# A scored with landmarks on the rows, its fold turned by DMA, and row-tiled products

## The chip, the cores and the metric

The kernel runs on one core of one Trainium2 chip. The metric is the time of one execution on the device in microseconds (us). Runs more than 1.5% above the fastest of the same kernel are called slow. PE is TensorE, ACT is ScalarE, DVE is VectorE, POOL is GpSimd, SP is the engine that issues most DMAs here. "Granted clock" is the share of PE's full clock that the profile shows as granted. SBUF is the memory that tiles lie in, PSUM the one that PE writes its products to. "The chain that ended last" is the work followed back from the last instruction, at each step to what it had waited for.

## The reference, cut to what matters

```python
# q, k, v: (8 batches, 8 heads, 576 rows, 64); m = 32 landmarks, each the mean of 18 rows
A  = softmax(scale * q    @ k_lm.T)      # 576 x 32 per head
Bm = softmax(scale * q_lm @ k_lm.T)      # 32 x 32
C  = softmax(scale * q_lm @ k.T)         # 32 x 576
Z  = six Newton steps towards the inverse of Bm
x  = A @ Z @ C @ v                       # heads side by side: 576 x 512 per batch
x1, x2, x3 = split(x @ w_proj)
y  = x1 * irfft(rfft(x2) * filter) * x3  # the transform runs along the 576 rows
out = y @ w_out
```

The transform of x2 is taken on A itself, 256 columns per batch (8 heads of 32), which is smaller than x2. The transform is split into even and odd frequencies, so it needs the sum and the difference of rows s and s+288 of A: the "fold". A is therefore needed twice: with rows s on the partitions, folded (AE, weights of the DFT), and turned, with (head, landmark) on the partitions (AT, for the products with G).

## The kernel before

It forms A with the rows on the partitions, 96 rows to a tile, and turns it on PE. Cuts are marked.

```python
def back(b):
    def scores(cc, src, t, dst):                       # 512 columns: 2 chunks x 8 heads x 32
        pc = ktile("pc")                               # PSUM, two buffers
        ...                                            # eight products of 64 columns
        nc.scalar.activation(dst[:, 2*cc:2*cc+2, :].rearrange("p c l -> p (c l)"),
                             pc[:R, :], AF.Exp, bias=0.0, scale=scale)
    for cc in range(3):
        scores(cc, qT, 0, eA)
        nc.vector.tensor_reduce(rA[...], eA[...], axis=AX.X, op=ALU.add)
        scores(cc, kT, 1, eC)
    ...                                                # 1/rA, A = eA * (1/rA), C @ v
    nc.vector.tensor_tensor(AE[:, 0], A[:, 0:3], A[:, 3:6], op=ALU.add)       # the fold
    nc.vector.tensor_tensor(AE[:, 1], A[:, 0:3], A[:, 3:6], op=ALU.subtract)
    ...
    for g in range(2):                                 # A turned on PE
        pt = ktile("ptA", F16)
        for c in range(NC):                            # NC = 6
            mm(pt[:, c*R:(c+1)*R], A[:, c, 128*g:128*g+128], identh[:R, :R], is_transpose=True, ...)
        nc.vector.tensor_copy(AT[:, g, :], pt[:, :S])

def gate(b, after):
    ...                                                # DFT, G = ZC @ w_proj, X, Y
    def conv(j, EO):                                   # three full products a parity
        for par in range(2):
            pi = wtile()
            for t in range(2):
                mm(pi[:, 0:HS], Y[:, par, t, P*j:P*j+P], IV[:, par, t, :], start=(t == 0), stop=False)
            mm(pi[:, 0:HS], Y2[:, P*(j%2):P*(j%2)+P], IV2[:, j//2, par, :], start=False, stop=True)
            nc.scalar.copy(EO[:, par, j%2], pi[:, 0:HS])
```

A batch passes a front (landmark means, first products), six Newton steps, `back` (above), and the gate; the instructions of up to four batches are woven together. Below, "front stretch" is the time in which fronts, scores, Newton steps and DFTs run, and "gate stretch" the rest of a batch.

The softmax here doesn't subtract the row's maximum and nothing guards it: scores larger than these inputs give would overflow.

Of the kernel before, what the change touches and what calls it, by code (L numbers as in the profile page):

```python
# [8 lines left out]
F32 = mybir.dt.float32  # L9
BF16 = mybir.dt.bfloat16  # L10
# [10 lines left out]
def kernel(  # L21
# [10 lines left out]
    nc = tc.nc  # L32
# [7 lines left out]
    NC = S // R  # L40
    HS = S // 2
    TW = HS + 16

    NPE = 2
    consts = ctx.enter_context(tc.tile_pool(name="consts", bufs=1))
# [39 lines left out]
    def load_q(b):  # L85
        qn = io.tile([R, H, NC, D], BF16, tag="qn", name="qn")
        for e in range(2):
            nc.gpsimd.dma_start(
                qn[:, :, 3 * e:3 * e + 3, :].rearrange("p h c d -> p h (c d)"),
                q[b].rearrange("h (e p c) d -> e p h (c d)", e=2, c=3)[e])  # L90
        loaded[b].append(qn)

    def load_v(b):
        vn = vbufs[b % NV]
        for i in range(2):
            nc.gpsimd.dma_start(  # L96
                vn[:, :, i].rearrange("p x c d -> p x (c d)"),
                v[b].rearrange("(x h) (p c) d -> h p x (c d)", h=2, c=NC)[i])
        vloaded[b] = vn

    def load(b):
# [5 lines left out]
    kc = big.tile([R, 2, TW], F32, tag="y", name="kc")  # L107
    nc.gpsimd.iota(kc[:, :, 0:P], pattern=[[1, 2], [2, P]], base=0, channel_multiplier=0,
                   allow_small_or_imprecise_dtypes=True)
    nrow = consts.tile([R, 3], F32, name="nrow")  # L110
    nc.gpsimd.iota(nrow, pattern=[[1, 3]], base=0, channel_multiplier=3,
                   allow_small_or_imprecise_dtypes=True)
    load_q(0)
# [8 lines left out]
    poolq = consts.tile([R, 16], BF16, name="poolq")  # L122
    nc.vector.memset(poolq, 1.0)
    select(poolq, [[-6, 16]], ALU.is_ge, 0.0, 0, 1)
    select(poolq, [[6, 16]], ALU.is_ge, 0.0, 5, -1)

# [7 lines left out]
    lmbufs = [consts.tile([P, 2, H, 2, m], BF16, name=f"lm{i}") for i in range(NL)]  # L134
# [5 lines left out]
    for tb in tbufs:  # L140
        for x in tb:
            nc.vector.memset(x[:, 24 * R:], 0.0)
    IV2 = consts.tile([P, 2, 2, HS], F16, name="IV2")

# [9 lines left out]
    for lb in lmbufs[1:]:  # L154
        fill(lb.rearrange("p t h c l -> p (t h c l)"), 4 * H * m, 0.0)
    fill(IV2.rearrange("p x y s -> p (x y s)"), 4 * HS, 0.0)
    off = big.tile([R, 2, TW], F32, tag="y", name="off")
# [6 lines left out]
    J = consts.tile([P, 2, 64], F16, name="J")  # L164
    JH = consts.tile([P, 2, 2, 64], F16, name="JH")
    mask2 = consts.tile([P, 2], F32, name="mask2")
    nc.vector.memset(J, 0.0)
    nc.vector.memset(mask2, 1.0)
    select(J, [[0, 2], [-1, 64]], ALU.not_equal, 1.0, 0, 1)
    select(J, [[0, 2], [-1, 64]], ALU.not_equal, 1.0, -64, 1)  # L170
    select(mask2, [[-64, 2]], ALU.is_ge, 0.0, 0, 1)
    select(mask2, [[64, 2]], ALU.is_ge, 0.0, 63, -1)
    for e in range(2):
        nc.vector.tensor_scalar(JH[:, e], J, mask2[:, e:e + 1], None, op0=ALU.mult)
# [5 lines left out]
    nc.vector.tensor_copy(blk4, mask4.unsqueeze(2).to_broadcast([P, 4, 32]))  # L180
    identh = consts.tile([P, P], F16, name="identh")
# [4 lines left out]
    def load_w(i):  # L186
# [3 lines left out]
    filt = big.tile([R, 2, 3, Dm], BF16, tag="G", name="filt")  # L190
    nc.gpsimd.dma_start(filt.rearrange("p e c j -> p e (c j)"),
                        moe_filter_fft.rearrange("(e p c) j -> p e (c j)", e=2, c=3))
# [3 lines left out]
    F = consts.tile([R, 3, 2, TW], F16, name="F")  # L196
    Ft = consts.tile([R, 3, 2, 2, 2, 16], F16, name="Ft")
# [4 lines left out]
    def tables_fwd():  # L202
# [5 lines left out]
        for c in range(3):  # L208
            t = big.tile([R, 2, TW], F32, tag="T", name="t", bufs=1)
            nc.vector.scalar_tensor_tensor(t, in0=kc, scalar=nrow[:, c:c + 1],  # L210
                                           in1=off, op0=ALU.mult, op1=ALU.add)
            u = big.tile([R, 2, TW], F32, tag="X", name="u")
# [25 lines left out]

    def front(b):
        kn, qn = loaded[b]  # L240
        lm = lmbufs[b % NL]
# [3 lines left out]
        for h in range(H):  # L245
            for cc in range(3):
                x = mm(pk[:, h * m:(h + 1) * m],  # L247
                       kn[:, h, 2 * cc:2 * cc + 2, :].rearrange("p c d -> p (c d)"),
                       poolk, start=(cc == 0), stop=(cc == 2), skip_group_check=True)
                if b in pins:  # L250
                    tc.keep_in_program_order(x)
        yield
        pq = ftile("pq")
        pq3 = pq[:, 0:384].rearrange("p (x h l) -> p x h l", x=3, h=H)
        for h in range(H):
            for cc in range(3):
                x = mm(pq3[:, cc, h, :],  # L257
                       qn[:, h, 2 * cc:2 * cc + 2, :].rearrange("p c d -> p (c d)"),
                       poolq, start=True, stop=True, skip_group_check=True)
                if b in pins:  # L260
                    tc.keep_in_program_order(x)
        Pk = sm.tile([P, H, m], F16, tag="Pk", name="Pk")
        nc.scalar.activation(Pk.rearrange("p h l -> p (h l)"), pk[:, 0:256], AF.Copy,
                             bias=0.0, scale=1.0 / blk)
        Pq = sm.tile([P, 3, H * 16], F16, tag="Pq", name="Pq")
        nc.scalar.activation(Pq.rearrange("p x l -> p (x l)"), pq[:, 0:384], AF.Copy,
                             bias=0.0, scale=1.0 / blk)
        yield
        pj = ftile("pj")
        pj4 = pj.rearrange("p (t h l) -> p t h l", t=2, h=H)  # L270
        Jf = J.rearrange("p a d -> p (a d)")
        mm(pj[:, 0:256], Jf, Pk.rearrange("p h l -> p (h l)"), start=True, stop=True,
           skip_group_check=True)
        for e in range(2):
            dst = pj4[:, 1, :, 16 * e:16 * e + 16]
            mm(dst, Jf, Pq[:, 2 * e, :], start=True, stop=False, skip_group_check=True)
            mm(dst, JH[:, e].rearrange("p a d -> p (a d)"), Pq[:, 1, :],
               start=False, stop=True, skip_group_check=True)
        nc.vector.tensor_copy(lm[0:64, :, :, 0, :], pj4[0:64])
        nc.scalar.copy(lm[64:128, :, :, 1, :], pj4[64:128])  # L280
# [6 lines left out]
        for g in range(2):  # L287
            for hh in range(4):
                h = 4 * g + hh
                mm(B2[32 * hh:32 * hh + 32, g, :], lm[0:64, 1, h, 0, :], lm[0:64, 0, h, 0, :],  # L290
                   start=True, stop=True, skip_group_check=True)
# [84 lines left out]
    def back(b):  # L376
        vn = vloaded.pop(b)
        lm = lmbufs[b % NL]
        kT, qT = tbufs[b % 2]

        def scores(cc, src, t, dst):
            pc = ktile("pc")
            pc4 = pc.rearrange("p (c h l) -> p c h l", c=2, h=H)
            for h in range(H):
                mm(pc4[:, :, h, :], src[:, (3 * h + cc) * R:(3 * h + cc) * R + P],  # L385
                   lm[:, t, h, :, :].rearrange("p c l -> p (c l)"),
                   start=True, stop=True, skip_group_check=True)
            nc.scalar.activation(dst[:, 2 * cc:2 * cc + 2, :].rearrange("p c l -> p (c l)"),  # L388
                                 pc[:R, :], AF.Exp, bias=0.0, scale=scale)

        eC = big.tile([R, NC, 256], BF16, tag="eC", name="eC", bufs=1)
        eA = big.tile([R, NC, 256], BF16, tag="eA", name="eA", bufs=1)
        rA = sm.tile([R, NC * H], F32, tag="rA", name="rA")
        for cc in range(3):
            scores(cc, qT, 0, eA)
            nc.vector.tensor_reduce(  # L396
                rA[:, 2 * H * cc:2 * H * (cc + 1)],
                eA[:, 2 * cc:2 * cc + 2].rearrange("p c (h l) -> p (c h) l", l=m),
                axis=AX.X, op=ALU.add)
            yield  # L400
            scores(cc, kT, 1, eC)
            yield


        nc.vector.reciprocal(rA, rA)
        rA2 = sm.tile([R, NC * H, 2], BF16, tag="rA2", name="rA2")
        nc.vector.tensor_copy(rA2, rA.unsqueeze(2).to_broadcast([R, NC * H, 2]))
        A = big.tile([R, NC, 256], F16, tag="A", name="A", bufs=1)
        nc.vector.tensor_tensor(
            A.rearrange("p c (h a t) -> p (c h) a t", a=16, t=2),  # L410
            eA.rearrange("p c (h a t) -> p (c h) a t", a=16, t=2),
            rA2.unsqueeze(2).to_broadcast([R, NC * H, 16, 2]), op=ALU.mult)
# [4 lines left out]
        for g in range(2):  # L417
            pv = ktile("pv")
            for c in range(NC):
                for x in range(2):  # L420
                    mm(pv[64 * x:64 * x + 64, 0:192],  # L421
                       eC[:, c, 128 * g + 64 * x:128 * g + 64 * x + 64],
                       vn[:, 2 * g + x, :, c, :], start=(c == 0), stop=(c == NC - 1),
# [10 lines left out]
        AE = big.tile([R, 2, 3, 256], F16, tag="AE", name="AE")  # L434
        nc.vector.tensor_tensor(AE[:, 0], A[:, 0:3], A[:, 3:6], op=ALU.add)
        nc.vector.tensor_tensor(AE[:, 1], A[:, 0:3], A[:, 3:6], op=ALU.subtract)
        att[b] = dict(AE=AE)
        yield
        pz = ktile("pz")
        RZ = solved.pop(b)  # L440
        pz4 = pz[:, 0:128].rearrange("p (x l) -> p x l", x=4)
        for g in range(2):
            for pp in range(2):
# [380 lines left out]
```

## Time and profile before

| kernel before | |
|---|---|
| time | 240.7 us median of 3 runs (240.68 to 240.97) |
| span of the profiled run, mean granted clock | 241.6 us, 0.961 |
| first factor product (G with AT) of batches 0 to 7, us from the start | 52.4, 81.9, 110.5, 135.5, 160.0, 184.5, 206.4, 223.2 |
| steps between them | 29.5, 28.5, 25.1, 24.5, 24.5, 21.9, 16.8 |

The steps are the clearest measure of a batch. The last ones have less of a next batch to prepare, so 16.8 us is a gate nearly alone.

Three windows of the kernel before: a front stretch, three steady batches, a gate nearly alone. After the window come its length and the busy time of each engine.

```profile
core 0: us, PE busy (x) PEld busy (x) DVE busy (x) ACT busy (x) POOL busy (x), PEclk, DMA share, GB/s
117.60:126.80 9.20, 8.88 (x163) 6.25 (x162) 7.22 (x22) 7.41 (x20) 2.30 (x3) 1.00 1.08 221
110.50:184.70 74.20, 73.62 (x880) 44.62 (x880) 60.42 (x158) 63.03 (x142) 4.98 (x7) 1.00 0.95 144
206.40:223.20 16.80, 16.72 (x129) 9.02 (x129) 10.72 (x18) 14.95 (x33) 0.00 (x0) 1.00 0.27 71
```

PE is busy 73.62 of 74.20 us.

Groups of instructions of the kernel before (busy us, mean ns of one, then idle time of the engine before them):

```profile
L396 DVE TENSOR_REDUCE rA<-eA 96x16 f32<-96x512 bf16 x24 | 16.2, 677 | 3.0 <-ACT eA L388 2.8
L388 ACT ACTIVATE eA<-pc 96x512 bf16<-96x512 f32 x24 | 14.6, 607 | 0.4 <-PE pc L385 0.3
...
L409 DVE TENSOR_TENSOR A<-eA,rA 96x1536 f16<-96x1536 bf16 x8 | 7.6, 947 | 0.0
L462 DVE COPY AT<-ptA 128x576 f16<-128x576 f16 x16 | 7.2, 447 | 3.9 <-PE ptA L460 3.9
L460 PE MATMUL ptA<-identh,A 96*128 96x96 f16 x96 | 7.0, 215 | 0.0
```

These are what the change takes out or replaces. The exp of A takes 607 ns for 512 columns.

What a change of PE's tile mode costs is seen in the chain of the kernel before. Its columns are start, length, engine, tile and line, and how many instructions.

```profile
126.77 0.55 PE w L537 x4
127.32 0.97 PE w L680 x4
...
129.51 0.86 PE w L680 x4
...
132.36 0.55 PE w L583 x16
132.91 0.97 PE w L680 x4
```

Four full 512-column products take 0.86 us among their own kind and 0.97 behind 64-column (L537) or 32-column (L583) products: 0.11 us for each change of mode.

### The profile page before, as it was taken

The page shows a single profiled execution, that of the slowest core. Times are in us where ns is not written, and L with a number is a line of the kernel's source. Part 1 is how long each engine was busy: PE and PEld are TensorE (multiplying, and loading weights), DVE is VectorE, ACT ScalarE, POOL GpSimd, SP SyncE. Part 2 cuts the span into 40 slices and gives each one's busy share as a digit, 9 for nine tenths or more (in the row PEclk, how much of TensorE's full clock was granted, in tenths as well). Part 3 has the DMA queues.
Part 4 walks back from the last instruction along what each step waited for, and adds up shares of the span by engine and source line. Part 5 has one row for each costly group of instructions (what it writes and reads, how often), then busy time and mean ns, then how long its engine had stood idle before and what let it go on. Part 6 is the DMA issues. An engine that isn't in the chain of part 4 may idle for free.

```text
span 241.6 us, 6421 instructions
## 1 busy us (share of the span) xinstructions
PE 223.4 (92%) x2547; PEld 134.6 (56%) x2547; DVE 182.4 (75%) x478; ACT 185.8 (77%) x407; POOL 37.7 (16%) x62
## 2 busy tenths in 40 slices
PE   7959769999999999999999999999999999999980
PEld 3537434666665667645754576457645664554630
DVE  8936943579978989896879777977797789567540
ACT  8663525888879878888878888788878987898850
POOL 7962310012203321040032001100000000000000
PEclk9967965999999999999999999999999999999998
DMA  5999999949999999999999996995015004305115
GB/s 73 195 210 196 208 202 198 172 80 176 165 149 167 218 196 154 177 191 146 171 217 140 165 230 152 115 157 173 3 47 152 0 3 107 89 4 150 48 42 153
DMA packets 61998, 33.78 MB, mean 140 GB/s; under 512 B 42320, under 2 KB 57680, under 8 KB 61968
## 3 DMA queue, kind: packets, MB, share of 16 engines
q0 software_dynamic: 27536, 16.85, 53.7%
q1 hardware_dynamic: 34432, 16.52, 36.1%
q8 instruction: 20, 0.33, 0.6%
q14 instruction: 10, 0.08, 0.1%
HBM read 33.69 MB, written 9.44 MB: 178 GB/s over the span
## 4 chain that ended last, share of the span: by engine, by line
PE 78%; DVE 9%; ACT 9%; issue 1%; DVEq 0%; ACTq 0%
PE w L612 12%; PE w L680 11%; PE w L639 6%; PE w L568 6%; PE w L537 6%; PE w L547 5%; PE pc L385 4%; PE pv L421 4%; PE pn L362 3%; PE w L641 3%; PE pq L257 2%; PE ptA L460 2%; PE w L504 2%; PE w L583 2%; PE pk L247 2%; ACT EO L643 2%
## 5 line engine op out<-in xcount | busy, mean ns | idle before, releaser
L680 PE MATMUL w<-wout,y 128*128 128x512 bf16 x128 | 33.4, 380 | 0.4 <-DVE y L658 0.4
L612 PE MATMUL w<-AT,G 128*128 128x512 f16 x128 | 32.8, 380 | 0.2
L541 ACT CAST G<-w 128x512 bf16<-128x512 f32 x48 | 25.5, 597 | 4.0 <-PE w L537 3.9
L617 DVE TENSOR_TENSOR gt<-w,x 128x512 bf16<-128x512 f32 x32 | 21.6, 685 | 9.0 <-ACT x L615 5.0
L643 ACT CAST EO<-w 128x288 bf16<-128x288 f32 x64 | 24.1, 403 | 2.8 <-PE w L641 2.8
L682 ACT COPY os<-w 128x512 f32<-128x512 f32 x32 | 18.5, 589 | 8.9 <-PE w L680 8.3
L639 PE MATMUL w<-IV,Y 128*128 128x288 f16 x128 | 25.0, 286 | 0.3 <-ACT EO L643 0.3
L573 DVE TENSOR_TENSOR T<-X,HH 128x2048 bf16<-128x2048 bf16 x16 | 19.5, 1220 | 7.1 <-ACT X L570 6.4
L615 ACT CAST x<-w 128x512 bf16<-128x512 f32 x32 | 19.0, 599 | 2.9 <-PE w L612 2.4
L537 PE MATMUL w<-wproj,ZC 128*64 128x512 bf16 x96 | 19.4, 400 | 0.0
L547 PE MATMUL w<-F,AE 96*128 96x304 f16 x96 | 19.2, 313 | 0.1
L680 PEld LDWEIGHTS <-y 128*128 128x128 bf16 x128 | 11.0, 97 | 14.5 <-issue 4.2
L570 ACT CAST X<-w 128x512 bf16<-128x512 f32 x32 | 17.9, 592 | 1.4 <-PE w L568 0.9
L396 DVE TENSOR_REDUCE rA<-eA 96x16 f32<-96x512 bf16 x24 | 16.2, 677 | 3.0 <-ACT eA L388 2.8
L641 PE MATMUL w<-IV,Y 128*128 128x288 f16 x64 | 18.3, 286 | 0.0
L568 PE MATMUL w<-G,Ah 128*128 128x512 bf16 x64 | 18.0, 382 | 0.0
L612 PEld LDWEIGHTS <-G 128*128 128x128 bf16 x128 | 11.0, 97 | 12.5 <-ACT G L541 4.0
L366 ACT CAST RZ<-pn 128x256 f16<-128x256 f32 x40 | 15.4, 386 | 2.8 <-PE pn L362 1.8
L96 POOL DMA_DIRECT2D vb<-in_v_dram x16 | 10.8, 678 | 41.0 <-PE w L547 25.1
L549 ACT CAST Ah<-w 128x304 f16<-128x304 f32 x32 | 12.8, 421 | 4.3 <-PE w L547 4.2
L362 PE MATMUL pn<-RZ 128*128 128x160 f16 (+1 forms) x96 | 13.7, 223 | 2.3 <-DVE RZ L367 1.7
L729 PE MATMUL w<-zero 128*128 128x512 bf16 (+1 forms) x55 | 14.2, 398 | 1.4 <-DVE zero L138 1.4
(152 smaller groups left out, 472.4 us busy)
## 6 DMA issues: line engine op xcount, KB each, us to landing
kn<-in_k_dram POOLq DMA_DIRECT2D x8, 576.0 KB, 9.7
qn<-in_q_dram POOLq DMA_DIRECT2D x16, 288.0 KB, 11.5
vb<-in_v_dram POOLq DMA_DIRECT2D x16, 288.0 KB, 9.7
out_dram<-os SPq DMA_DIRECT2D x24, 192.0 KB, 2.5
out_dram<-os SPq DMA_DIRECT2D x16, 128.0 KB, 2.4
wproj<-in_moe_w_proj_dram POOLq DMA_DIRECT2D x3, 512.0 KB, 14.8
out_dram<-os SPq DMA_DIRECT2D x24, 64.0 KB, 2.1
out_dram<-o SPq DMA_DIRECT2D x16, 64.0 KB, 2.1
```

Of the source, the lines that this page charges most:

```text
L362: mm(pn2[:, g, lo:160], RZ[:, g, 0:128], RZ[:, g, lo:160], start=True, stop=True, skip_group_check=True)
L537: mm(pg[64 * pp:64 * pp + 64, :], part["ZC"][:, 2 * g + pp, :, :].rearrange("p h l -> p (h l)"), wparts[jb][:, 2 * g + pp, :], start=True, ...
L541: nc.scalar.copy(G[:, g, Dm * jb:Dm * (jb + 1)], pg)
L547: mm(pf[:, 0:TW], part["AE"][:, par, c, 128 * g:128 * g + 128], F[:, c, par, :], start=(c == 0), stop=(c == 2))
L568: mm(px, Ah[:, g, par, 128 * t:128 * t + 128], G[:, g, Dm:2 * Dm], start=(g == 0), stop=(g == 1))
L573: nc.vector.tensor_tensor(T, X.unsqueeze(2).to_broadcast([P, 2, 2, Dm]), HH[:, par], op=ALU.mult)
L612: mm(px, G[:, g, lo:lo + P], part["AT"][:, g, 0:512], start=(g == 0), stop=(g == 1))
L617: nc.vector.tensor_tensor(gt[:, j, 0:512], px, x1, op=ALU.mult)
L639: mm(pi[:, 0:HS], Y[:, par, t, P * j:P * j + P], IV[:, par, t, :], start=(t == 0), stop=False)
L641: mm(pi[:, 0:HS], Y2[:, P * (j % 2):P * (j % 2) + P], IV2[:, j // 2, par, :], start=False, stop=True)
L643: nc.scalar.copy(EO[:, par, j % 2], pi[:, 0:HS])
L680: mm(po, y[:, j, i0:i0 + P], wout[:, j, :], start=(j == 0), stop=(j == 3))
```

## The change

The intent: make the scores of A directly with (head, landmark) on the rows, so that no PE transpose and no wide DVE reduction is needed. Row sums and the spreading of their reciprocals become small PE products. The fold becomes sums and differences of the two halves of a row of AT, and only the folded A is turned, by DMA, from the second batch on. Products that use 32 or 64 of the array's rows are tiled by rows, so that several can run together. The core of the diff, with cuts marked:

```diff
-        for e in range(2):
-            nc.gpsimd.dma_start(qn[:, :, 3*e:3*e+3, :]..., q[b].rearrange("h (e p c) d -> ...", e=2, c=3)[e])
+        nc.gpsimd.dma_start(qn..., q[b].rearrange("h (p c) d -> p h (c d)", c=NC))
 ...
+        def scores_a(g):
+            pa = [ktile("pa") for _ in range(2)]
+            for pos in range(4):
+                for c2 in range(2):
+                    h = head(g, pos)
+                    mm(pa[c2][32*pos:32*pos+32, 0:HS], la[64*c2:64*c2+64, h, :],
+                       qT[64*c2:64*c2+64, h*HS:(h+1)*HS], ...)
+            for c2 in range(2):
+                nc.scalar.activation(eA[:, g].rearrange("p (r c x) -> p c x r", x=2, c=3)[:, :, c2, :],
+                                     pa[c2][:, 0:HS].rearrange("p (c r) -> p c r", r=R),
+                                     AF.Exp, bias=0.0, scale=scale)
 ...
+        # row sums: pr[...] = SU x eA, twelve 32-column products; rA2 = 1/pr
+        for g in range(2):
+            pb = [ktile("pb") for _ in range(2)]
+            ...            # pb = SB x rA2, six products of 32 rows
+            for c2 in range(2):
+                view = lambda t: t[:, g].rearrange("p (c x r) -> p c x r", x=2, r=R)[:, :, c2, :]
+                nc.vector.tensor_tensor(view(AT), view(eA), pb[c2]..., op=ALU.mult)
+        ...                # At = AT[:, :, 0:288] +- AT[:, :, 288:576]
+        if b >= NPA:       # NPA = 1
+            nc.sync.dma_start_transpose(AE, At)
+        else:
+            ...            # nine PE transposes, two copies
 ...
         def conv(j, EO):
+            pi = [wtile() for _ in range(2)]
             for par in range(2):
                 for t in range(2):
                     mm(pi[par][:, 0:HS], Y[:, par, t, ...], IV[:, par, t, :], start=(t == 0), stop=False)
-                mm(pi[:, 0:HS], Y2[:, ...], IV2[:, j//2, par, :], start=False, stop=True)
+            for par in range(2):
+                p0 = 64*(j//2) + 32*par
+                mm(pi[par][:, 0:HS], Y2[p0:p0+32, ...], IV2[p0:p0+32, :], start=False, stop=True)
 ...
-            store(i0, P, os)                   # rows 3p+c of each half
+            nc.sync.dma_start(out[b, i0:i0+P, :], os)
```

The DFT's last 32 rows become row-tiled products like those of conv, G is made of eight tiles of 64 rows by 32 columns, and the landmark means of 512-column products. The order of rows changes too: q now comes as rows 6p+c, and the columns of A are put back into natural order.

## The prediction

> **What bounds it now.** The page gives TensorE (PE) 92% busy, ScalarE (ACT) 77%, VectorE (DVE) 75%, DMA at nine tenths for two thirds of the span; the chain of waits that ended last is 78% PE, 9% DVE, 9% ACT. From the timeline: 62 us for the first batch, then some 24.5 us a batch (first L612 at 110.5, 135.7, 160.2, 184.7), 16.8 us for the last ones, which have no next batch to prepare. The window of three steady batches (110.5 to 184.7) shows PE busy 73.6 of 74.2 us, ACT 63.0, DVE 60.4. In its gate stretch, about 16 us, PE issues back to back; in the front stretch (117.6 to 126.8: pooling, scores, Newton, DFT) the products' own spacing sums to about 7 of 9 us and the chain goes PE to ACT and back.
>
> **What the change does, per batch.**
> DVE: out go row-sum reduction (3x677 ns), reciprocal and copy (437+201), A product (947), fold (543+546), AT copies (2x447), masked ZC (418), lm (680): 6.7 us. In come a reciprocal (est. 0.75), four 288-column products from PSUM (est. 0.46 each, between the 425 ns of 256 and the 685 of 512), folds (est. 1.15), ZC, lm and small ones: est. 5.0. Saves 1.7.
> ACT: exp of A from 3x607 to 4x403 (the 128x288 copy); Pk, Pq, lm (385+492+581) become Pk and la (est. 590+371). Saves 0.7.
> PE: matmuls of different column groups already start 3 ns apart in the trace (64-column pairs, 32-column fours), and each change of column mode costs about 106 ns (the 512-column matmul lands 322 ns after a tiled one, 216 after its own kind). [...] So g_part falls from about 0.65 to 0.44 us, three times (-0.6); twelve A transposes of 43 ns go (-0.5); pooling with 512-column products, pj, row sums, spreading of the reciprocals and pz add about 1.5, mostly switches. Conv (24 products of 122 ns to 20 slots) and DFT (12 of 130 to 10) save 0.75 if row-tiled pairs run together and the switch between full and row-tiled is free, as 96-row and 128-row ones mix freely now[...]. Net PE: between -0.4 and +1.3 us.
> DMA: q comes in half as many packets; each AE transpose (seven, 295 KB) has a whole gate to land in.
>
> **On the critical path.** The gate stretch gains from g_part and the removed transposes until ACT (14.9 of 16.8 us at the end) stops it. The front stretch gains through ACT and DVE, and loses PE's switches. I estimate 0.5 to 0.8 us less for each of six batches, 1 at the start, 1 to 2 at the end: about 6 us.
>
> **Predicted:** 235 us, 8 in 10 between 228 and 244. Faster by over 2%: 0.54; within 2%: 0.33; slower: 0.13.
>
> **What would show it.** DVE busy near 170 us, ACT near 178; PE as busy as now; the step from batch to batch near 23.8; row-tiled conv pairs ending some 3 ns apart; no chain piece waiting for the AE transpose.
>
> **What would make it wrong.** [...] pairs of PSUM buffers taken at once that make PE wait for both exps; AE transposes queued behind stores; or a front stretch bound by ACT's chain more than I think, so that 228 comes out.

The 106 ns are from the trace. The bad case of the row-tiled products: if a change between full and row-tiled products costs what a change of column mode does, conv and DFT lose 0.5 us a batch instead of saving 0.75, and the time is about 240 us or more. The sum: per batch 1.7 us saved on DVE, 0.7 on ACT, between -0.4 and +1.3 on PE (plus is time added); on the critical path 0.5 to 0.8 us for each of six batches, 1 at the start and 1 to 2 at the end, about 6 us, from 240.7 to 235.

That 96-row and 128-row products mix freely is in the trace of the kernel before: from 110 us on, a 512-column product lands 217 to 219 ns after a 96-row one and 216 after its own kind. Where an estimate names no line, its working is not on record. The same trace has, to set beside them: a reciprocal of 1 column 148 ns and of 48 columns 437 (the 0.75 us is for 96), the folds 543 and 546 ns (the 1.15 us), ACT copies of 512 columns 592 ns and of 256 columns 371 (the 590 and 371 ns). The 0.44 us for g_part and the 1.5 us that PE adds are estimates.

## More of the kernel before

The page of the kernel before: busy time of each engine, the granted clock in 40 equal slices (tenths of full speed), and the chain that ended last.

```profile
PE 223.4 (92%) x2547; PEld 134.6 (56%) x2547; DVE 182.4 (75%) x478; ACT 185.8 (77%) x407; POOL 37.7 (16%) x62
...
PEclk9967965999999999999999999999999999999998
...
PE 78%; DVE 9%; ACT 9%; issue 1%; DVEq 0%; ACTq 0%
```

PE sets the pace, and from the eighth slice on its clock is full (1.00 from 42 to 241 us).

## The result and the profile after

The changed kernel took 306.36 us (median of 4 runs, 305.79 to 320.39), the kernel before 240.83 us beside it. Over fast runs the ratio is 1.271 (95% interval 1.268 to 1.274). Ratios here are the mean time of one kernel's fast runs over that of the other's of the same rounds, so not quite the ratio of the medians quoted.

| | before | after |
|---|---|---|
| span of the profiled run | 241.6 us | 303.9 us |
| mean granted clock | 0.961 | 0.861 |
| first factor product of batch 0 | 52.4 | 60.3 |
| steps from batch to batch | 29.5, 28.5, 25.1, 24.5, 24.5, 21.9, 16.8 | 41.9, 40.3, 32.7, 31.7, 32.9, 29.2, 17.8 |
| from the first factor product of batch 7 to the end | 18.4 | 17.2 |

The page of the changed kernel, the same three lines:

```profile
PE 267.4 (88%) x2501; PEld 127.7 (42%) x2516; DVE 175.5 (58%) x484; ACT 200.5 (66%) x407; POOL 35.3 (12%) x60
...
PEclk9978599999788999569965999599956996899998
...
PE 69%; ACT 12%; DVE 8%; DMA 7%; issue 2%; POOL 1%; POOLq 0%; DVEq 0%
```

DVE has 7 us less, where some 12 were expected (near 170). ACT has 15 more instead of 8 less. The clock, full from the eighth slice on before, now falls to half over and over, about once a batch (0.50 from 154.5 to 168.2, 188.6 to 198.8 and 219.3 to 233.0 us, and 1.00 between these).

Three windows of the changed kernel: the half-clock part of one batch, three steady batches, a gate nearly alone.

```profile
core 0: us, PE busy (x) PEld busy (x) DVE busy (x) ACT busy (x) POOL busy (x), PEclk, DMA share, GB/s
154.50:168.20 13.70, 13.37 (x111) 6.07 (x113) 6.69 (x27) 8.50 (x19) 0.00 (x0) 0.50 0.89 160
142.40:239.70 97.30, 92.37 (x857) 42.34 (x862) 56.52 (x156) 68.21 (x142) 4.21 (x6) 0.81 0.49 104
268.90:286.70 17.80, 17.52 (x139) 7.83 (x140) 10.55 (x18) 14.57 (x33) 0.00 (x0) 1.00 0.19 67
```

PE looks busy in the first of them (13.37 of 13.70 us) only because its products take about twice as long (the eight of L398 0.54 us at 157.6, against 0.23 to 0.25 at full clock). A mean granted clock of 0.81 over three batches means that about 38% of that time ran at half speed (the three stretches at 0.50 are 37.6 of 97.3 us). The gate alone, at full clock, is only 1.0 us longer than before.

Groups of the changed kernel:

```profile
L388 ACT ACTIVATE eA<-pa 128x288 bf16<-128x288 f32 x32 | 34.4, 1222 | 1.2 <-PE pa L384 1.0
...
L676 ACT CAST EO<-w 128x288 bf16<-128x288 f32 x64 | 22.5, 403 | 10.9 <-PE w L673 9.1
L571 PE MATMUL w<-F,AE 128*128 128x304 f16 x64 | 17.6, 369 | 5.8 <-DMA AE<-At 5.8
L435 DVE TENSOR_TENSOR AT<-eA,pb 128x288 f16<-128x288 bf16 x32 | 14.1, 451 | 15.5 <-PE pb L431 15.4
...
L384 PE MATMUL pa<-qT,la 64*32 64x288 bf16 x128 | 10.0, 295 | 9.4 <-ACT eA L388 9.4
```

The exp of A takes 1222 ns for 288 columns, while another ACT operation on 288 columns, from PSUM to bf16 as well, takes 403. PE waits 9.4 us for it in front of the next scores, and 5.8 us for the folded A to come back from DMA.

The chain of waits of the changed kernel between 50 and 125 us, the pieces of ACT and DMA:

```profile
62.53 2.09 ACT eA L388 x2
65.04 2.09 ACT eA L388 x2
...
74.32 7.75 DMA AE<-At
...
93.25 3.91 ACT eA L388 x4
...
107.12 13.93 DMA AE<-At
```

The second and third batch wait 7.75 and 13.93 us for the DMA transpose. The mean busy share that the trace gives for DMA is 1.23 and 1.29 in these two stretches (it goes over 1), against 0.49 in the three steady batches. In later batches no such piece is left.

The chain in a gate of the changed kernel, for the row-tiled products of conv (L673):

```profile
177.95 0.49 PE w L669 x4
178.44 0.23 PE w L673 x2
178.67 0.61 PE w L669 x4
179.27 0.23 PE w L673 x2
```

The pair runs together: its two products end 2 to 5 ns apart in the trace. But the pair takes 0.23 us, not 0.12, and the four full products behind it 0.61, not 0.49. Entering and leaving the row-tiled mode cost about 0.1 us each, together more than the slot of 0.12 us that the pair saves.

So there are three suspects:

- **S, steps in the output.** The 12-byte steps of the exp's output (it writes neighbouring columns six bf16 elements apart) make it three times slower (1222 against 403 ns). That holds PE in the front stretch (9.4 us in all), and the waits, so the guess, bring PE's clock down to half.
- **D, the DMA turn.** The AE transposes land late in the first batches (waits of 7.75 and 13.93 us).
- **M, modes.** Mode switches of the many small tiled products (about 0.1 us each).

### The profile page after: what moved, and what is told of

Read it like the earlier page. It is cut to its first block, busy times and chain, and to the rows that moved or that the text cites. A ratio compares the mean times of both kernels' runs of the same rounds, so it can differ in the third digit from the quotient of the medians.

```text
span 303.9 us, 6348 instructions
## 1 busy us (share of the span) xinstructions
PE 267.4 (88%) x2501; PEld 127.7 (42%) x2516; DVE 175.5 (58%) x484; ACT 200.5 (66%) x407; POOL 35.3 (12%) x60
## 3 DMA queue, kind: packets, MB, share of 16 engines
q0 software_dynamic: 21680, 16.85, 39.6%
## 4 chain that ended last, share of the span: by engine, by line
PE 69%; ACT 12%; DVE 8%; DMA 7%; issue 2%; POOL 1%; POOLq 0%; DVEq 0%
PE w L702 10%; PE w L642 8%; ACT eA L388 7%; DMA AE<-At 7%; PE w L598 6%; PE w L669 5%; PE w L561 4%; PE pv L468 4%; PE w L571 4%; PE pc L398 3%; PE pn L357 3%; PE pk L257 2%; PE pb L431 2%; PE w L673 2%; PE w L575 2%
## 5 line engine op out<-in xcount | busy, mean ns | idle before, releaser
L702 PE MATMUL w<-wout,y 128*128 128x512 bf16 x118 | 35.9, 411 | 2.8 <-issue 1.8
L388 ACT ACTIVATE eA<-pa 128x288 bf16<-128x288 f32 x32 | 34.4, 1222 | 1.2 <-PE pa L384 1.0
L642 PE MATMUL w<-AT,G 128*128 128x512 f16 x128 | 33.5, 381 | 0.2
L669 PE MATMUL w<-IV,Y 128*128 128x288 f16 x128 | 24.4, 287 | 0.1
L435 DVE TENSOR_TENSOR AT<-eA,pb 128x288 f16<-128x288 bf16 x32 | 14.1, 451 | 15.5 <-PE pb L431 15.4
L571 PE MATMUL w<-F,AE 128*128 128x304 f16 x64 | 17.6, 369 | 5.8 <-DMA AE<-At 5.8
L598 PE MATMUL w<-G,Ah 128*128 128x512 bf16 x59 | 19.9, 433 | 0.0
L362 DVE TENSOR_TENSOR RZ<-RZ,pn 128x64 f16<-128x64 f16 x48 | 10.2, 212 | 15.4 <-ACT RZ L361 11.2
L561 PE MATMUL w<-wproj,ZC 64*32 64x512 bf16 x192 | 18.5, 450 | 0.1
L384 PE MATMUL pa<-qT,la 64*32 64x288 bf16 x128 | 10.0, 295 | 9.4 <-ACT eA L388 9.4
L357 PE MATMUL pn<-RZ 128*128 128x160 f16 (+1 forms) x96 | 16.8, 256 | 0.6 <-DVE RZ L323 0.6
```

Of the source, the lines that this page charges most:

```text
L357: mm(pn2[:, g, lo:160], RZ[:, g, 0:128], RZ[:, g, lo:160], start=True, stop=True, skip_group_check=True)
L388: nc.scalar.activation(eA[:, g].rearrange("p (r c x) -> p c x r", x=2, c=3)[:, :, c2, :], pa[c2][:, 0:HS].rearrange("p (c r) -> p c r", r= ...
L561: mm(pg[g][32 * pos:32 * pos + 32, :], part["ZC"][64 * g:64 * g + 64, pos, :], wparts[jb][64 * g:64 * g + 64, head(g, pos) // 2, :], start ...
L571: mm(pf[par][:, 0:TW], part["AE"][:, 4 * par + 2 * g + c, :], F[:, c, par, :], start=(c == 0), stop=False)
L598: mm(px, Ah[:, g, par, 128 * t:128 * t + 128], G[:, g, Dm:2 * Dm], start=(g == 0), stop=(g == 1))
L642: mm(px, G[:, g, lo:lo + P], part["AT"][:, g, 0:512], start=(g == 0), stop=(g == 1))
```

## The experiments

Twelve kernels ran. Each was compared with runs of the kernel before on the same chip. All passed the comparison with the reference.

### e1: exp packed, the steps moved to DVE

```diff
-  nc.scalar.activation(eA[:, g].rearrange("p (r c x) -> p c x r", x=2, c=3)[:, :, c2, :], ...
+  nc.scalar.activation(eA[:, g].rearrange("p (c x r) -> p c x r", x=2, c=3)[:, :, c2, :], ...
-  view(AT), view(eA), pb...
+  turn(AT), view(eA), pb...        # turn: the (r c x) pattern, 12-byte steps
```

> The changed kernel with one thing turned round: the exp of A writes its columns packed (runs of 96) and the product that makes AT, on DVE, puts them into their order (steps of 12 bytes) instead. The result stays right. Theory S (the exp's 12-byte steps made it 1222 ns instead of 403, which holds PE in the front stretch and drops its clock to half): exp of A near 403 ns, the half-clock parts of the steady batches mostly gone, time 250 to 270. Rival M (mode switches of the tiled products and pairs of PSUM buffers are what costs) and rival D (waits for the turned A by DMA): 290 or more. If DVE is slowed by such steps as ACT is, the AT product goes from 451 ns to over 1000 and the time stays above 280.

Measured: 283.73 us median (275.01 to 289.68; one run fast, three slow, so no ratio is given). The groups of e1:

```profile
L436 DVE TENSOR_TENSOR AT<-eA,pb 128x288 f16<-128x288 bf16 x32 | 33.2, 1150 | 2.4 <-PE pb L431 2.2
...
L388 ACT ACTIVATE eA<-pa 128x288 bf16<-128x288 f32 x32 | 12.3, 420 | 1.3 <-PE pa L384 1.0
```

The cost moved with the steps: the exp fell from 1222 to 420 ns, and the DVE product rose from 451 to 1150. It was the warned-of case, though the time decides little: the one fast run, 275.0 us, lies between the two forecasts (250 to 270, and over 280), and the trace is of the slowest run. In that trace the steady steps fell to 27.2 us, and no half-clock part was left in them. So S is a cost of writing in steps, not of ACT.

### e2: the kernel before, exp of A in steps

```diff
+            if t == 0:
+                to = to.rearrange("p (k s) -> p s k", s=8)
+                fr = fr.rearrange("p (s k) -> p s k", s=8)
```

> The kernel before, with only the exp of A writing each of its 512 columns in steps of 16 bytes within the same block (wrong result on purpose). Theory S: 3.6 ns a column as in the changed kernel, so about 1850 ns instead of 607, 30 us more of ACT, time 265 to 290 and half-clock parts in the steady batches. If steps of the output are harmless and the slow exp came of something else in the changed kernel (two PSUM banks filled at once, row-tiled products): 607 ns and 241 us.

Measured: 305.22 us (303.78 to 305.85), ratio 1.267 (95% interval 1.261 to 1.273; the record classes e2, and e3 below, as "unclear", although both intervals lie far from 1), at a mean granted clock of 0.81 to 0.83. (The landmark order in A is scrambled; the result passed all the same. That A is nearly uniform for these inputs may be why; it was not looked into.) From the groups and the page of e2:

```profile
L392 ACT ACTIVATE eA<-pc 96x512 bf16<-96x512 f32 x24 | 58.6, 2442 | 0.8 <-PE pc L385 0.5
...
L385 PE MATMUL pc<-lm,qT 128*128 128x64 bf16 x192 | 12.8, 213 | 26.1 <-ACT eA L392 26.0
```

```profile
PEclk9976579966995897599755995589758995799996
```

One output pattern, in a kernel that has nothing else of the change, costs 64 us and brings the same saw-tooth of the clock. I had expected 1850 ns and at most 290 us; steps of 16 bytes cost more than those of 12 (2442 ns for 512 columns is 4.8 ns a column, 1222 for 288 is 4.2). There is no DMA turn, no row tile and no new mode switch here. S alone is enough for a loss of this size.

### e3: A's fold turned by PE in all batches

```diff
-    NPA = 1
+    NPA = 8
```

> The changed kernel with the folded A turned by PE in every batch, none by DMA. Rival D: the 21.7 us that the chain gives to the AE transposes go, with the half-clock parts behind them: time 275 to 285. Theory S: the waits of the second and third batch go (about 8 and 14 us), but nine transposes of 54 ns and two copies of 0.5 us a batch come back, and the steady batches stay at 31 to 32 us: 290 to 300.

Measured: 301.62 us (298.86 to 308.94, two runs fast), ratio 1.243 (95% interval 1.236 to 1.250). The clock keeps its saw-tooth:

```profile
PEclk9979589999995799999958995599859985999998
```

The steps became 36.7, 36.3, 32.8, 33.5, 32.2, 30.3, 17.8: the second and third batch gained 5.2 and 4.0 us, the steady ones nothing. D is real but small while S is there. The fast runs are in the range given for S.

### e4: the cost of steps by itself

A block behind the end of the kernel before runs exp on ACT and copies on DVE from the same PSUM tile to bf16, 256 columns each, in different steps.

> The kernel before with a block behind its end that measures by itself, three times each: exp on ACT of 256 columns from PSUM written as bf16 in steps of 1, 2, 3, 4, 6 and 8 elements, the changed kernel's own pattern (3 runs of 96 in steps of 6), a copy from SBUF that reads in steps of 8; and on DVE a copy from PSUM written in the same steps. Theory S: ACT near 370 ns at step 1 and near 950 at steps 6 and 8, the read in steps cheap. Open: from which step on, and whether DVE minds; if DVE shows the same the AT product of e1 will be slow.

This kernel did not build (a slice of the pattern had the wrong length) and did not run. The mended one:

> The probe as meant before (a slice was mended): the kernel before with a block behind its end that measures, three times each, exp on ACT of 256 columns from PSUM written as bf16 in steps of 1, 2, 3, 4, 6 and 8 elements, the changed kernel's pattern (3 runs of 96 in steps of 6), a copy from SBUF read in steps of 8, and on DVE a copy from PSUM written in the same steps. Theory S, now with 2442 ns for 512 columns in steps of 8, 1040 to 1222 ns for 288 in steps of 6, and 1150 ns on DVE in steps of 6: about 370 ns at step 1, 900 to 1250 at steps 6 and 8 on ACT, about as much on DVE, the strided read near 400. Open: whether the cost grows with the step or comes at once at step 2.

Its groups; L802 to L807 are ACT and L810 to L815 are DVE, in steps of 1, 2, 3, 4, 6 and 8 elements, and L808 and L816 are the changed kernel's pattern. L809 is a copy on ACT that reads SBUF in steps of 8 and writes packed:

```profile
L807 ACT ACTIVATE tt<-w 128x256 bf16<-128x256 f32 x3 | 3.9, 1302 | 0.1
...
L808 ACT ACTIVATE tt<-w 128x288 bf16<-128x288 f32 x3 | 3.4, 1125 | 0.1
L816 DVE CAST tt<-w 128x288 bf16<-128x288 f32 x3 | 3.3, 1113 | 0.1
L806 ACT ACTIVATE tt<-w 128x256 bf16<-128x256 f32 x3 | 3.1, 1020 | 0.1
L814 DVE CAST tt<-w 128x256 bf16<-128x256 f32 x3 | 3.0, 1006 | 0.1
L805 ACT ACTIVATE tt<-w 128x256 bf16<-128x256 f32 x3 | 2.2, 737 | 0.1
...
L809 ACT ACTIVATE tt<-tt 128x256 bf16<-128x256 bf16 x3 | 2.0, 652 | 0.1
L804 ACT ACTIVATE tt<-w 128x256 bf16<-128x256 f32 x3 | 1.8, 597 | 0.1
...
L803 ACT ACTIVATE tt<-w 128x256 bf16<-128x256 f32 x3 | 1.4, 456 | 0.1
L811 DVE CAST tt<-w 128x256 bf16<-128x256 f32 x3 | 1.3, 444 | 0.1
L810 DVE CAST tt<-w 128x256 bf16<-128x256 f32 x3 | 1.3, 425 | 19.5 <-ACT tt L809 19.5
L802 ACT ACTIVATE tt<-w 128x256 bf16<-128x256 f32 x3 | 1.2, 384 | 11.8 <-DVE tt L816 11.7
```

Both engines show the same course: 384, 456, 597, 737, 1020 and 1302 ns on ACT, 425, 444, about 580, about 720, 1006 and 1290 on DVE, so within 20 ns of each other from step 2 on. Step 2 costs little (384 to 456 ns on ACT, 425 to 444 on DVE). From there each further element of step adds 141 ns to 256 columns, 0.55 ns a column. The changed kernel's pattern takes 1125 ns by itself, so most of its 1222 in the kernel is explained without PE or pairs of PSUM buffers; 97 ns are not. From these lines an estimate for any step from 2 on is 174 ns + 0.55 ns x columns x step; it gives some 2430 ns for e2's exp (512 columns, step 8), where 2442 were measured. The read in steps was expected near 400 ns and took 652: half of what the same step costs in a write. The probe has no packed copy from SBUF to set beside it.

### e5: nothing in steps

q is loaded in the order of the kernel before (rows 3p+c of each half), so that chunks of 96 lie as the fold wants them and every output is packed. The DFT tables, the filter's rows, the weights of q's means and the stores follow that order.

```diff
-  nc.gpsimd.dma_start(qn..., q[b].rearrange("h (p c) d -> p h (c d)", c=NC))
+  for e in range(2): nc.gpsimd.dma_start(qn[:, :, 3*e:3*e+3, :]..., q[b].rearrange("h (e p c) d -> ...")[e])
-  eA[:, g].rearrange("p (r c x) -> p c x r", x=2, c=3)[:, :, c2, :]
+  eA[:, g].rearrange("p (c x r) -> p c x r", x=2, c=3)[:, :, c2, :]
   # nrow, poolq, filt, store: as that order asks
```

> The changed kernel with no step in any output: q is loaded in the order of the kernel before (rows 3p+c of each half, so the chunks of 96 fall into place by themselves), exp and AT product both write runs of 96; tables, filter rows and stores follow that order, as they did before the change. Result right. Theory S: exp near 410 ns and the AT product near 450, steady batches 24 to 26 us at full clock, what is left is the AE wait of the first batches and about 1 us a batch of mode switches: 250 to 265 us. If something else in the change costs as much, steady batches stay at 27 or more and the time above 268.

Measured: 285.59 us median (281.86 to 293.65; two fast, two slow, no ratio given). The steps are 39.2, 45.7, 26.1, 26.1, 26.1, 24.5, 17.8. The steady part did what S says: 26.1 us at full clock, against 32 to 33. The total missed my range of 250 to 265, because the third batch got worse: PE idled 15.2 us for AE in all, and the clock was halved there for 17.1 us. D grew. A likely reason is that without S the first batches come earlier to the stretch in which DMA is full (the second gate starts at 96.0 us, where it was 102.1; in the changed kernel the share of DMA is 0.78 from the first gate to the second and 1.27 from there to the third); but q now also comes in smaller packets (as in the kernel before, where the queue that loads it moved 16.85 MB in 27536 packets, against 21680 in the changed kernel). The two were not separated.

### e6: packed, three batches turned by PE

```diff
-    NPA = 1
+    NPA = 3
```

> The one above with the folded A of the first three batches turned by PE instead of DMA. Theory D for the start (DMA is full there, so the AE transposes land 8 to 14 us after issue): 5 to 12 us less than the one above, 242 to 254 us, the chain free of DMA. If that wait only covered others: within 2 us of it.

Measured: 273.48 us (271.64 to 276.8), ratio 1.133. It is faster, but not what I expected: the first two steps are now 30.1 and 32.4, and the wait has moved to the fourth batch (step 37.9, with 17.1 us of half clock), the first one still turned by DMA.

### e7: as e6, conv and DFT as full products

```diff
-  mm(pi[par][:, 0:HS], Y2[p0:p0+32, ...], IV2[p0:p0+32, :], ...)
+  mm(pi[par][:, 0:HS], Y2[:, ...], IV2[:, j//2, par, :], ...)          # zero-padded
-  mm(pf[par][:, 0:TW], part["AE"][p0:p0+32, 8, :], F[p0:p0+32, 2, par, :], ...)
+  mm(pf[par][:, 0:TW], part["AE"][:, 8, :], F2[:, par, g, :], ...)     # zero-padded
```

> The one above with the row-tiled products of conv and DFT made full again (zero-padded tables, as the kernel before had them for conv), all else kept. Theory M in small (each row-tiled pair costs two switches of about 105 ns and saves one slot of 122 to 130 ns, six times a batch): about 0.5 us a batch, 3 to 5 us in all. If the switches hide behind ACT: no difference within 1 us.

Measured: 261.45 us (258.82 to 265.12), ratio 1.077. The gain of 12 us (13.6 in the means of fast runs) is more than M allows. Most of it is the fourth batch again (37.9 to 26.7 us). Elsewhere the steady steps went from 26.1 to 25.8, and the gate alone from 17.8 to 17.2. Two causes were mixed here, so e8 and e11 take them apart. Why the DMA turn held PE for 5.7 us in e6 and for 0.9 here stays open.

### e8: as e7, every batch turned by PE

```diff
-    NPA = 3
+    NPA = 8
```

> The packed kernel with full conv and DFT products, and the folded A turned by PE in all eight batches. In e7 the chain still gave 12.25 us to one AE transpose. Theory D: it goes, and with it 3 to 8 us, against about 0.5 us a batch of PE for nine more transposes in batches three to seven: 254 to 260 us. If that wait was only the last of several that end together: 261 to 264.

Measured: 260.68 us (260.31 to 264.02), ratio 1.086. Nothing gained: steps 32.3, 33.0, 26.4, 26.4, 26.4, 24.2, 17.2. The AE wait that the chain of e7 showed (12.25 us) only covered what ended at the same time: PE itself idled 0.9 us for AE there. The nine transposes cost 0.6 us a batch.

### e11: as e8, conv and DFT row-tiled

> Between e6 and e8 two things are mixed: e7 lost 12 us against e6, but most of it in one batch whose wait for the turned A by DMA went (step 37.9 to 26.7 us). This is the packed kernel with all of A turned by PE and conv and DFT still row-tiled, so against e8 it differs in the row-tiled products alone. Theory M in small: 0.3 us a steady step and 0.6 us a gate without a next batch, as e6 and e7 showed: 3 to 5 us over e8's 260.7, so 263 to 266, no batch step above 34. If row tiling itself did more than that (it also changes when the transposes are issued): 268 or more.

Measured: 264.32 us (263.85 to 275.33), ratio 1.097. In medians this is 3.6 us above e8, as expected, in the means of fast runs 2.7, and the 95% intervals of the two ratios overlap (1.091 to 1.103, 1.079 to 1.094). The steps are 30.1, 33.0, 26.7, 26.6, 26.6, 24.9, 17.8. From the third batch's gate on they sum to 2.2 us more than those of e8 (122.7 against 120.5). The other 1.5 of the 3.7 us between the profiled spans are 0.3 at the end and 1.2 before that gate: there e11's first gate came 3.5 us later (with 17.1 us of half clock at the start, against 10.2), and its first step was 2.2 shorter. So the row tiling of conv and DFT costs about 2 us in the later batches and saves nothing; what it costs at the start is not shown. e11 is the changed kernel without S and D. Its window of three steady batches:

```profile
120.80:200.70 79.90, 79.88 (x889) 39.09 (x888) 57.83 (x159) 61.88 (x145) 4.97 (x7) 1.00 0.81 133
```

### e9: as e8, the reciprocals spread by full products

```diff
-  SB[p0:p0+32, j] ... rA2[p0:p0+32, :]         # 32-row tiles
+  SB[:, 2*g+c2, j] ... rA2                     # zero-padded, 128 rows
```

> The one above with the spreading of the reciprocals (pb) as full 128-row products on a zero-padded table instead of 32-row tiles. In a steady batch of e7, PE never idles, its mode changes 43 times (14 in the kernel before) at some 105 ns each, and pb is behind about eight of these. Theory M (what is left over the kernel before is mode switches): 5 to 7 switches fewer a batch, 0.4 to 0.7 us, so steady steps near 0.5 us shorter than in e8 and 3 to 5 us in all. If ACT or the chain of waits sets the pace now: no difference.

Measured: 259.45 us (259.0 to 259.58), ratio 1.078. The steady steps fell from 26.4 to 25.8, as expected, but the time only by 1.2 us: the first batch began 2.1 us later (with 17.1 us of half clock at the start, against 10.2).

Counted in the traces, PE changes its tile mode in one steady batch so often:

| kernel | switches in a steady batch | its step, us |
|---|---|---|
| before | 14 | 24.5 |
| e11 (packed, row-tiled) | 54 | 26.6 |
| e8 (conv and DFT full) | 43 | 26.4 |
| e9 (reciprocals full as well) | 35 | 25.8 |

PE idles at most 0.33 us in these batches. With 0.105 us a switch, before to e11 are 40 switches, 4.2 us by estimate. By this count the products themselves became about 2.1 us cheaper (4.2 less the 2.1 us by which the step grew), and the switches took twice that. From e8 to e9, eight switches fewer would give 0.84 us; the full products gave 0.6 net. From e11 to e8, eleven fewer would give 1.16 us; the zero-padded products gave 0.2 net.

### e10 and e12: the kernel before, with A turned by DMA

The one idea of the change that takes time from PE without a new mode was tried alone, on the kernel before, with A laid out so that one transpose turns it.

```diff
+        if b >= NPA:                                     # e10: 3, e12: 1
+            nc.sync.dma_start_transpose(AT.rearrange("p g (c r) -> p (g c) r", r=R),
+                                        A.rearrange("p g c l -> p (g c l)"))
-        for g in range(2): ...                           # twelve PE transposes, two copies: only for b < NPA
```

> The kernel before with one idea of the change alone: from the fourth batch on, A is turned by DMA instead of twelve PE transposes and two DVE copies (eA and A laid out by head group so that one transpose does it; all else kept, result right). PE has no idle time in its steady batches, the transposes take 0.52 us of it a batch, and A-turned is read only late in the gate. So five batches lose about 0.5 us each: 236.5 to 239.5 us. If the DMA lands late or DVE and ACT, not PE, set the pace: 240.5 or more.

Measured: 241.2 us median of 6 runs (237.8 to 245.2), three fast (237.8 to 238.56) and three slow. Over fast runs the ratio is 0.990 (95% interval 0.983 to 0.998). By the 2% line this is "same", but it is faster clear of the noise. The steady steps are 24.0 us where they were 24.5: the 0.52 us of PE transposes, as expected. In its fast runs it is the fastest kernel, by about 1%. Over all its runs it is not: half of them were slow, and the median of all six is that of the kernel before beside it (241.04 us).

> e10 (the kernel before with A turned by DMA from the fourth batch on, 238 us in its fast runs) with the second and third batch turned by DMA too. If the DMA lands in time there as well, although it is full in those batches: two more batches lose 0.5 us each, 236.5 to 238. If it lands late, as the folded A of the changed kernel did in those batches: the factors of the second or third batch wait, 239 or more.

Measured: 253.68 us (249.73 to 257.1), ratio 1.044. Its second step, to the third batch, is 44.9 us, where e10 has 28.4. This trace is of the slowest run (257.1 us); the three fast ones, of mean 251.4, lost some 6 us less, and still 13 against e10. The chain of e12 in that step, its longest pieces:

```profile
87.65 10.11 SPq L354
97.85 14.38 DMA AT<-A
```

First the issuing queue stood 10.11 us at a K/Q transpose, then A took 14.38 us to land, against a median of 3.4 in e10. What waited for it was the next batch's product A on DVE (16.2 us idle), as A has one buffer, which the DMA was still reading (the product starts at 112.33 us, 0.10 after the landing). The same transposes that help from the fourth batch on cost 12 us or more in the second and third, where DMA is full (at nine tenths or more in every slice of e12's page from 6 to 160 us; that is past the third batch too, so why they land late just there is not shown).

## Why the prediction was wrong

Point by point:

- **The step that failed** is the ACT term, "exp of A from 3x607 to 4x403 (the 128x288 copy)", and from it "Saves 0.7". The 403 ns belong to a copy that writes packed; the new exp writes in 12-byte steps. Measured: 1222 ns. The exp got 4x1222 less 3x607, 3.1 us a batch more instead of 0.2 less; ACT as a whole was busy 1.8 us a batch more (200.5 against 185.8 us) instead of 0.7 less. The output pattern stood in the diff and I priced the instruction by its shape alone.
- **The clock that followed was not in the prediction at all.** That PE might wait for both exps of a pair of PSUM buffers stood among its risks, but with PE at full clock. The front stretch was fed through ACT and two PSUM buffers. With PE waiting in pieces of 0.62 and 0.42 us there, its clock halved for 10 to 14 us a batch. In the trace the longest PE gap between 151 and 156 us is 0.62 us (in all PE idled 1.05 of the 3.5 us from 151 on), and the clock is at half from 154.5 on. That steps in the exp bring the clock down is shown by e2; that they do it through these waits is the reading of what follows what in the trace, which no run tested.
- **How much of it is S:** with A turned by PE in both, the fast runs of e3 (mean 299.2) and e11 (264.2) differ in the steps, and in the row order that goes with it: 35 us. Of the 6.2 us by which their steady steps differ (32.8 and 26.6), PE's idle time is at most 1.5: in the three steady batches of e3 it idled 1.5, 1.0 and 1.3 us. They ran at half clock for 10.2, 13.7 and 10.2 us, and half of that, 5 to 7 us, is an estimate of the most that this cost. So by this estimate most of the loss is the clock, and not the waits themselves; the two were not separated by a run.
- **"Each AE transpose has a whole gate to land in"** was wrong for the second and third batch (7.75 and 13.93 us of waits in the chain). Its size depends on S: turning on PE is worth 7 us while the steps are there (fast means 306.2 and 299.2) and 19 when they are gone (e5 283.5, e11 264.2). Two losses that hide behind each other do not add up.
- **Net PE "between -0.4 and +1.3 us"** named the right cause, the switches, and as its own risk that those of the row-tiled products are not free. They are not: 0.10 to 0.11 us each way (in conv at full clock a pair lands 224 ns after a full product, and a full one 229 ns after a pair, against 122 among full ones), as for the column modes. The term was mis-sized: the step of e11 is 2.1 us over that of before, 0.5 of it the PE transposes that it has again (e6, turned by DMA there as in the change, has 26.1, 1.6 over). So PE got 1.6 us a batch more, beyond the bad end of the range (1.3, with plus for time added). Its sign was known as the risk and weighed too lightly; the forecast of 235 us needed the good end.
- **Right were** the DVE items (AT product 451 ns for an estimated 460, reciprocal 756 for 750), row-tiled pairs ending some 3 ns apart (2 to 5), and G (eight tiles together: their ends lie within 21 to 45 ns). The DVE items saved nothing, because DVE did not set the pace.

Of the 62 us between the profiled spans, e11 leaves 21 (262.7 against 241.6): so steps and the DMA turn together are about 41. Of these 21 us, 10 are lost before the third batch's gate and 11 after it. Of the latter about 2 are the row tiling of conv and DFT; most of the rest is by its count of switches the other small tiled products, and e9 shows that for one of them. What stays open is the start: e8 and e9, without steps, DMA turn and row tiles in conv and DFT, still lose 9 to 10 us there. The traces say that it is not waiting: up to the third gate PE idles 9.3 us in e8 and 10.2 in the kernel before, but it is busy 110.3 us against 100.3, with less of it at half clock (10.2 against 17.1). So it is more work on PE; which of the small products and of the tables made at the start carry it was not tried.

## What to carry to other kernels

Price an instruction by its access pattern, not by its shape alone: look for the innermost step of every output in a diff before taking a duration from a similar line of the trace (here 1222 ns, not 403). Where PE is the bound, a small tiled product costs its switches first (here 0.10 to 0.11 us each), so count mode changes per batch, and put zero-padded full products where a tile stands alone between full ones (in e8 and e9 that gave 0.2 and 0.6 us a batch). Look at the clock too: here waits of about half a microsecond in the densest engine went with 10 to 14 us at half clock, which by estimate cost more than the waits (in e3 at most 5 to 7 us a batch, where PE idled 1.0 to 1.5).
